# Three of four accumulation banks stream their moving columns in another order

## The chip, the cores and the metric

The kernel runs on one core of one Trainium2 chip. The core has TensorE (PE, which multiplies a weight tile that it loads against moving columns that it streams), VectorE (DVE), ScalarE (ACT), GpSimd (POOL) and SyncE (SP); here the last two mostly issue transfers. SBUF is the working memory of 128 partitions, PSUM holds eight banks of 512 f32 per partition, into which TensorE sums.

The metric is the device time of one execution in microseconds (us). The kernel before takes 709.25 us, the median of three runs (709.15 to 709.4).

## The reference

The reference mixes two branches of a layer on the same input x, of 2048 rows by 512:

```python
a = einsum("bsd,ed->bse", x, dft_hid_re); b = einsum("bsd,ed->bse", x, dft_hid_im)
A = einsum("ts,bse->bte", dft_seq_re, a) - einsum("ts,bse->bte", dft_seq_im, b)
gate = x @ w1; up = x @ w3                  # (2048 x 512) @ (512 x 1376)
B = (silu(gate) * up) @ w2
g = sigmoid((x * gate_w).sum(-1, keepdims=True))
out = g * A + (1 - g) * B
```

All arrays are f32. What matters for the change is the first product of the second branch, gate and up for the first 128 columns of w1 and w3.

## The kernel before, in words

The kernel works in stages. First comes the gate-and-up stage: for each chunk of 128 columns of w1 and w3 it forms silu(x w1) times x w3, transposed, and stores it in DRAM (`hsp`). Then come the products P with the sequence DFT, with w2 and with the hidden DFT, which fill most of the time. Almost all products use a scheme with seven block products in place of eight, whose operands are sums and differences of blocks (T1 to T4 of x, the forms `wa` and `wb` of the weights). Each f32 operand is split in two parts, a high part in the format fp32r, which ScalarE (or once VectorE) makes by a copy (`high`), and a low part, the rest, which VectorE makes by a subtraction (`low`). A product is then three matmuls: high by high, high by low, low by high (`mm3`, line 119).

The instructions of each engine are issued in the order in which the code is written; the kernel asks for a manual schedule, and engines wait for each other by semaphores. Loads go through SyncE's queue, stores mostly through GpSimd's.

The change lies in the very first chunk of the first stage, which is computed undivided: eight block products, no sums, since its operands are then ready as soon as they are loaded. Its result has four blocks, C00, C01, C10 and C11, each 128x512 in a PSUM bank of its own (`C[i, j]`). The first index tells gate (0) from up (1), the second the block of 512 rows of x. The function `half` issues half of one block's sum: six matmuls of 128x128 weights by 128x512 moving columns (line 432), two row blocks times three combinations of high and low. The moving operand is `xp(r, v)`: 512 neighbouring f32 of `XO[0]` (blocks B11, B21, B22 of x) or of the tile `b12`. Every bank gets `half` twice, first with start, then to add.

The order in the code is: eleven warm-up matmuls on a constant (line 407, tile `wps`), splits of the first operands, C00, C10, C00 again, C10 again, C01, C11, C01 again, C11 again, and then the first products X1, Y1, X2 and so on of the divided chunks (`prod1`, `prod2`, line 119). Between them, ScalarE applies Silu to C00 into the tile `s1` (line 466) and to C01 into `g1` (line 482), and VectorE multiplies `s1` by C10 into the first half of `h0` (line 472) and `g1` by C11 into the second (line 490). GpSimd's queue stores each half of `h0` (`store_h`, line 327). On ScalarE and VectorE these four instructions stand between splits (lines 108 and 111) and sums (line 207) of operands that later products need: behind line 466, the splits of the weights of chunks 1 and 2; behind line 472, the sum T2, the low parts `wa` of chunks 1 and 2, and the low part of T2.

Of the kernel before, what the change touches and what calls it, by code (L numbers as in the profile page):

```python
# [9 lines left out]
AF = mybir.ActivationFunctionType  # L10
ALU = mybir.AluOpType

P = 128
# [19 lines left out]
def fnet_swiglu_gate_kernel(  # L33
# [20 lines left out]
    nc = tc.nc  # L54
# [25 lines left out]
    def bank(k, name):  # L80
        return psum.tile([P, 512], F32, tag=f"ps{k}", name=name)
# [131 lines left out]
    def split_xo(g, k):  # L213
        split(*xo_parts(g, k))
# [62 lines left out]
    def prod1(n):  # L277
        x = bank(n % 4, f"X{n}")
        prod(x, n, 0, 0, True)
        return x  # L280
# [41 lines left out]
    def store_h(n, k, h):  # L322

        c, g = ITEMS[n]
        j = min(c % (NP2 - 1) if c < NC - 1 else NP2 - 1, NP2 - 1)
        b = 2 * (NP2 - 1 <= c < NC - 1)
        nc.gpsimd.dma_start(hsp[g, b + k, j // 2, :, j % 2 * 512 : (j % 2 + 1) * 512], h)  # L327
# [90 lines left out]
    b12, a21 = zt[0].rearrange("p h a n -> p h (a n)"), zt[1][:, :, 0]  # L418
    C = {(i, j): bank((0, 4, 6, 7)[2 * i + j], f"C{i}{j}") for i in range(2) for j in range(2)}

    def half(i, j, w, x, start):

        wp = lambda h, sl: a21[:, h, sl] if w is None else WA[0][:, h, w, sl]
        xp = lambda q, h: b12[:, h, q * 512 : (q + 1) * 512] if x is None else XO[0][:, h, x, q, :]
        hh, lh, hl = (0, 0), (1, 0), (0, 1)
        order = [(r, *p) for r in range(2) for p in ((hh, hl, lh) if w is None else (hh, lh, hl))]
        if w == x == 0:
            order = [(r, *p) for some in ((hh, lh), (hl,)) for r in range(2) for p in some]  # L430
        for n, (r, u, v) in enumerate(order):
            nc.tensor.matmul(C[i, j], wp(u, slice(r * P, (r + 1) * P)), xp(r, v),  # L432
                             start=start and n == 0, stop=not start and n == 5)

    def xo_half(k, q):
# [3 lines left out]
    s1 = s1p.tile([P, 512], F32, tag="s1", name="s1_0")  # L439
    g1 = u4p.tile([P, 512], F32, tag="u4", name="g1_0")  # L440
    h0 = hp.tile([P, 1024], F32, tag="h", name="h0")
# [10 lines left out]
    split_by_both(*xo_half("B11", 0))  # L452
    split(*xo_half("B11", 1))
    half(0, 0, 0, 0, True)
    split(a21[:, 0], a21[:, 1], WS[0][:, 3])
    half(1, 0, None, 0, True)
    high(*wa_parts(0, 1, 3)[::2])
    low(*wa_parts(0, 1, 2))
    split_by_both(*xo_half("B21", 0))
    split(*xo_half("B21", 1))  # L460
    low(*wa_parts(0, 2, 3))
    half(0, 0, 1, 1, False)
    split(b12[:, 0], b12[:, 1], ST[0, "B12"])
    half(1, 0, 2, 1, False)
    split_xo(0, "B22")
    nc.scalar.activation(s1, C[0, 0], AF.Silu)
    half(0, 1, 0, None, True)
    WS.pop(0)
    load_w(4)
    sum_xo(0, "T1", t1)  # L470
    half(1, 1, None, None, True)
    nc.vector.tensor_mul(h0[:, :512], s1, C[1, 0])
    store_h(0, 0, h0[:, :512])
    sum_xo(0, "T2", ST[0, "B11"])
    half(0, 1, 1, 2, False)
# [3 lines left out]
    half(1, 1, 2, 2, False)  # L479
    free(*zt)  # L480
    split_xo(0, "T2")
    nc.scalar.activation(g1, C[0, 1], AF.Silu)
    x1 = prod1(1)
    sums_wb(1)
    high(*xo_parts(0, "T1")[::2])
# [99 lines left out]
    for n in range(NI):  # L585
        if n in W2_AT:
            p = W2_AT.index(n)
# [4 lines left out]
        if n in A1_AT:  # L592
            p = A1_AT.index(n)
# [9 lines left out]
    n = NI - 1 - LOOK  # L603
# [348 lines left out]
    for i, (src, sp, p) in enumerate(late):  # L952
        blk, b = 1 + i // 2, i % 2
        n = (17, 24)[b]
# [84 lines left out]
```

## Time and profile before

| | |
|---|---|
| median of three runs | 709.25 us |
| profiled execution, first to last instruction | 707.2 us |
| TensorE busy | 702.7 us, 99% of the span |
| VectorE busy | 605.3 us, 86% |
| ScalarE busy | 370.1 us, 52% |
| instructions of TensorE | 3089 matmuls and as many weight loads |
| share of line 432 in the chain that ended last | 2% |
| mean granted TensorE clock | 0.999 of full |

The page of the profile prints the span of the profiled execution and no other time of it. The chain that ended last follows the work back from the last instruction to what released it. The duration printed for one matmul runs until its modelled end and overlaps the next one; the distance of two starts tells how long the engine is taken up. "C<-xo,wa" is an instruction that writes tile C and reads `xo` and `wa`; PEld is the weight load, which overlaps the matmul before it.

### The profile page before, as it was taken

What the parts mean: (1) busy time and instruction counts of PE and PEld (TensorE: products, weight loads), DVE (VectorE), ACT (ScalarE), POOL (GpSimd) and SP (SyncE); (2) the same over time, 40 slices, a digit from 0 to 9 for tenths busy, and PEclk for the clock granted to TensorE, in tenths of its full rate; (3) what the DMA queues carried; (4) which work ended last, traced back from release to release, by engine and by line L of the source; (5) the groups of instructions that cost most, each with busy time, mean ns of one, the idle gap of its engine ahead of it and who ended that gap; (6) DMA issues with size and microseconds to landing.
All of it is one profiled execution on the core that took longest, in us unless ns stands there. A gap on an engine that the chain in (4) does not pass through costs nothing.

```text
span 707.2 us, 8607 instructions
## 1 busy us (share of the span) xinstructions
PE 702.7 (99%) x3089; PEld 579.2 (82%) x3089; DVE 605.3 (86%) x737; ACT 370.1 (52%) x480; POOL 64.2 (9%) x118
## 2 busy tenths in 40 slices
PE   9999999999999999999999999999999999999997
PEld 6888888888888888888888888888888888888886
DVE  7989978887679999877999689969997896898985
ACT  6666555655446754454554454544555454455452
POOL 0011111211010000000110001100110000000000
PEclk9999999999999999999999999999999999999999
DMA  7665546589997566712595238914999971873932
GB/s 282 239 261 228 214 181 255 184 320 352 419 410 273 212 208 237 277 60 89 181 388 220 90 131 322 335 59 180 389 418 416 355 272 53 301 286 134 320 120 89
DMA packets 45547, 172.54 MB, mean 244 GB/s; under 512 B 5312, under 2 KB 5696, under 8 KB 41664
## 3 DMA queue, kind: packets, MB, share of 16 engines
q1 hardware_dynamic: 32608, 118.63, 45.7%
q0 software_dynamic: 12608, 52.97, 18.9%
q8 instruction: 24, 0.39, 0.2%
q10 hardware_dynamic: 288, 0.39, 0.2%
q14 instruction: 19, 0.16, 0.1%
HBM read 114.82 MB, written 57.16 MB: 243 GB/s over the span
## 4 chain that ended last, share of the span: by engine, by line
PE 99%; DVE 0%; ACT 0%; issue 0%
PE P L119 69%; PE X L119 16%; PE Z L119 8%; PE Y L119 4%; PE C L432 2%; PE wps L407 1%; DVE zc L829 0%; ACT zc L827 0%
## 5 line engine op out<-in xcount | busy, mean ns | idle before, releaser
L119 PE MATMUL P<-zo,a 128*128 128x512 f32 x1344 | 304.8, 389 | 0.0
L119 PEld LDWEIGHTS P<-zo,a 128*128 128x128 f32 x1344 | 252.3, 188 | 52.4
L108 ACT ACTIVATE zo<-B 128x1024 fp32r<-128x1024 f32 (+1 forms) x182 | 189.6, 1045 | 190.6 <-PE P L119 101.2
L111 DVE TENSOR_TENSOR zo<-B,zo 128x1024 fp32r<-128x1024 f32 (+1 forms) x182 | 218.0, 1204 | 48.7 <-ACT zo L108 48.2
L119 PE MATMUL P<-zo,H 128*128 128x512 f32 x468 | 106.2, 389 | 0.0
L119 PEld LDWEIGHTS P<-zo,H 128*128 128x128 f32 x468 | 87.8, 188 | 18.2
L675 DVE TENSOR_TENSOR B<-B,B 128x1024 f32<-128x1024 f32 (+1 forms) x78 | 92.9, 1191 | 0.1
L119 PE MATMUL X<-xo,wb 128*128 128x512 f32 x378 | 92.7, 389 | 0.0
L119 PEld LDWEIGHTS X<-xo,wb 128*128 128x128 f32 x378 | 70.9, 188 | 14.7
L119 PE MATMUL P<-zo,Y 128*128 128x512 f32 x336 | 76.3, 389 | 0.0
L119 PEld LDWEIGHTS P<-zo,Y 128*128 128x128 f32 x336 | 63.1, 188 | 13.1
L327 POOL DMA_DIRECT2D hsp<-h x42 | 23.1, 550 | 127.3 <-DVE h L381 76.1
L119 PE MATMUL X<-xo,wa 128*128 128x512 f32 x126 | 32.0, 389 | 0.0
L119 PE MATMUL Y<-xo,wa 128*128 128x512 f32 x126 | 32.0, 389 | 0.0
L119 PE MATMUL Z<-xo,wb 128*128 128x512 f32 x126 | 32.0, 389 | 0.0
L119 PE MATMUL Z<-xo,wa 128*128 128x512 f32 x126 | 32.0, 389 | 0.0
L678 DVE TENSOR_TENSOR B<-B,B 128x1024 f32<-128x1024 f32 x26 | 31.7, 1220 | 0.0
L904 ACT ACTIVATE zu<-P 128x512 f32<-128x512 f32 x32 | 19.1, 598 | 20.4 <-PE P L119 20.4
L375 DVE TENSOR_TENSOR u<-u,X 128x512 f32<-128x512 f32 x21 | 14.4, 688 | 16.8 <-PE X L119 16.8
L119 PEld LDWEIGHTS Y<-xo,wa 128*128 128x128 f32 x126 | 23.6, 188 | 4.9
L119 PEld LDWEIGHTS X<-xo,wa 128*128 128x128 f32 x126 | 23.6, 188 | 4.9
L119 PEld LDWEIGHTS Z<-xo,wb 128*128 128x128 f32 x126 | 23.6, 188 | 4.9
(137 smaller groups left out, 552.2 us busy)
## 6 DMA issues: line engine op xcount, KB each, us to landing
B<-cc SPq DMA_DIRECT2D x64, 512.0 KB, 6.3
hsp<-h POOLq DMA_DIRECT2D x42, 256.0 KB, 3.6
B<-hsp SPq DMA_DIRECT2D x20, 512.0 KB, 10.5
wbsp<-wb POOLq DMA_DIRECT2D x8, 1024.0 KB, 4.2
wb<-wbsp SPq DMA_DIRECT2D x8, 1024.0 KB, 7.5
B<-zsp SPq DMA_DIRECT2D x16, 512.0 KB, 8.4
H<-w2sp SPq DMA_DIRECT2D x6, 1024.0 KB, 9.2
ws<-w SPq DMA_DIRECT2D x11, 512.0 KB, 5.2
```

What stands on the lines that cost most here:

```text
L108: nc.scalar.activation(hi, src, AF.Copy)
L111: nc.vector.tensor_sub(lo, src, hi.bitcast(F32))
L119: nc.tensor.matmul(ps, u, v, start=first and n == 0, stop=last and n == 2, skip_group_check=chain)
L327: nc.gpsimd.dma_start(hsp[g, b + k, j // 2, :, j % 2 * 512 : (j % 2 + 1) * 512], h)
L375: nc.vector.tensor_add(u4, u4, x)
L407: nc.tensor.matmul(wps, warm[:, :P], warm, start=True, stop=True)
L432: nc.tensor.matmul(C[i, j], wp(u, slice(r * P, (r + 1) * P)), xp(r, v), start=start and n == 0, stop=not start and n == 5)
L675: nc.vector.tensor_add(t, t, RAW[blk, b, q][:, :n])
L678: nc.vector.tensor_sub(t, RAW[blk, "B12", q], t)
L904: nc.scalar.activation(U[name][:, r], ps[r], AF.Copy)
```

## The change

A bank no longer holds its 512 columns in their natural order. For three of the four banks, the matmul streams the moving columns in another order (`ordered`), and writes them into the bank one after another as they come. The view of the bank (`held`) is only a matching shape, and its addresses still run from front to back.

- C00: halves by turns. Columns 0, 256, 1, 257, and so on: each step is 256 elements (1024 bytes) forwards or 255 back.
- C10: even, then odd. Columns 0, 2, 4, ..., 510, then 1, 3, 5, ..., 511: a step of 8 bytes.
- C01: runs of 16 columns, that is 64 bytes, by turns from the first and the second half: 0 to 15, 256 to 271, 16 to 31, and so on.
- C11: as before.

The instructions that read these banks put the columns back: the Silu of C00 and the Silu of C01 write `s1` and `g1` in the order of the bank, so that these tiles are natural again, and the multiply with C10 reads `s1` and writes `h0` in the order even, then odd. The weights, the number of matmuls and their sequence stay.

```diff
+    ORDERS = {(0, 0): ("p (a n) -> p n a", "p (n a) -> p n a", {"a": 2}),
+              (1, 0): ("p (n a) -> p a n", "p (a n) -> p a n", {"a": 2}),
+              (0, 1): ("p (a b n) -> p b a n", "p (b a n) -> p b a n", {"a": 2, "n": 16})}
+
+    def ordered(i, j, v):
+
+        f = ORDERS.get((i, j))
+        return v.rearrange(f[0], **f[2]) if f else v
+
+    def held(i, j):
+        f = ORDERS.get((i, j))
+        return C[i, j].rearrange(f[1], **f[2]) if f else C[i, j]
+
...
-            nc.tensor.matmul(C[i, j], wp(u, slice(r * P, (r + 1) * P)), xp(r, v),
+            nc.tensor.matmul(held(i, j), wp(u, slice(r * P, (r + 1) * P)), ordered(i, j, xp(r, v)),
                              start=start and n == 0, stop=not start and n == 5)
...
-    nc.scalar.activation(s1, C[0, 0], AF.Silu)
+    nc.scalar.activation(ordered(0, 0, s1), held(0, 0), AF.Silu)
...
-    nc.vector.tensor_mul(h0[:, :512], s1, C[1, 0])
+    nc.vector.tensor_mul(ordered(1, 0, h0[:, :512]), ordered(1, 0, s1), held(1, 0))
...
-    nc.scalar.activation(g1, C[0, 1], AF.Silu)
+    nc.scalar.activation(ordered(0, 1, g1), held(0, 1), AF.Silu)
```

## The prediction

> **What bounds the kernel now.** I read the page first for the busy shares and the chain, then the waits of the TensorE side, then the chain in order of time over the first 30 us, then the instructions of the first undivided chunk one by one.
>
> ```profile
> span 707.2 us, 8607 instructions
> ...
> PE 702.7 (99%) x3089; PEld 579.2 (82%) x3089; DVE 605.3 (86%) x737; ACT 370.1 (52%) x480; POOL 64.2 (9%) x118
> ...
> PE 99%; DVE 0%; ACT 0%; issue 0%
> ...
> PEld L407 <- issue: 3.3, 10, 0.7
> PEld C L432 <- ACT xo L108: 0.6, 1, 0.6
> PEld C L432 <- DVE xo L111: 0.2, 1, 0.2
> ```
>
> The chain that ended last is TensorE for 99% of the span. The waits of the weight loads (the last three lines: waiter, releaser, us in total, times, longest) are three in the whole program, all before 7 us: the warm-up, the first matmul of bank C00, and its last. After that no matmul waits for anything. So whatever a matmul of the changed function takes longer goes to the end of the kernel undiminished, and nothing behind it can absorb it.
>
> ```profile
> 0.78 4.85 PE wps L407 x11
> 5.63 11.04 PE C L432 x48
> 16.67 1.36 PE X L119 x6
> ...
> 27.55 2.49 PE X L119 x11
> ```
>
> This is the chain in order of time (start, us, what; the last line is cut by its window). Six matmuls of 128x512 f32 take 1.36 us, so one follows another at 227 ns, here as everywhere. The 48 of line 432 take 11.04 us, 230 ns each. The duration of 389 ns that the groups print for one is its latency, and overlaps its neighbours; the spacing is the price.
>
> **The span against the time.** The sum is made against the profiled span of 707.2 us; the page prints no other time for that execution. The median of the three runs, 709.25, lies 2.05 us above it, and I keep those 2.05 us as they are: the change touches neither the launch nor the end.
>
> **The change part by part.** No instruction, wait, DMA or queue entry is added, removed or moved. Three things change: the addresses from which 36 matmuls stream their moving columns (12 for each of C00, C10, C01; C11 keeps its order), the addresses to which two Silu activations write, and all SBUF addresses of one multiply. The matmuls go on writing their PSUM bank front to back, since only the meaning of the columns changes, and the two activations and the multiply go on reading the bank front to back.
>
> *The matmuls.* Their places in time (start, us, engine, line, operation, out<-in, shapes, count), taken from narrow and wide windows of the timeline:
>
> ```profile
> 5.30 0.66 PE L432 MATMUL C<-xo,wa 128*128 128x512 f32 x1
> ...
> 5.80 0.62 PE L432 MATMUL C<-xo,wa 128*128 128x512 f32 x2
> ...
> 6.71 0.42 PE L432 MATMUL C<-xo,wa 128*128 128x512 f32 x1
> ...
> 6.96 0.62 PE L432 MATMUL C<-xo,a 128*128 128x512 f32 x2
> ...
> 8.34 2.88 PE L432 MATMUL C<-xo,wa 128*128 128x512 f32 x12
> 11.06 1.52 PE L432 MATMUL C<-b,wa 128*128 128x512 f32 x6
> 12.42 1.52 PE L432 MATMUL C<-b,a 128*128 128x512 f32 x6
> 13.78 2.88 PE L432 MATMUL C<-xo,wa 128*128 128x512 f32 x12
> ```
>
> In the order of the code these are: C00 (5.30 to 6.71), C10 (6.96), C00 and C10 again (8.34), C01 (11.06), C11 (12.42), C01 and C11 again (13.78). What a matmul costs when its moving columns are not neighbours no row of this trace shows: every moving operand of the kernel is read in runs of 512 neighbours. So I bound it.
>
> Lower bound. The warm-up matmuls show the array at half its later pace:
>
> ```profile
> 1.16 0.15 PEld L407 LDWEIGHTS <-const-bfloat16-1.0 128*128 128x128 bf16 x1 [0.28 <-issue]
> ...
> 4.57 0.15 PEld L407 LDWEIGHTS <-const-bfloat16-1.0 128*128 128x128 bf16 x1 [0.28 <-issue]
> ```
>
> Eight steps in 3.41 us are 426 ns each; half of that, 213 ns, is the least I can take from rows for 512 columns. Against 227 ns, 14 ns for each of 36 matmuls could be had at most if the spacing held some reading stall that another order avoids: -0.5 us. I see no reason for such a stall, and take no gain.
>
> Upper bound. If a fetch always brings four neighbouring columns and the contiguous stream of 227 ns is already limited by fetches, evens and odds would use half of each fetch (454 ns) and halves by turns a quarter (908 ns), while 64-byte runs (16 columns) would use all. That is +681 ns for a C00 matmul and +227 ns for a C10 one.
>
> What I take for each order, by the row it is nearest to:
> - C00, halves by turns: each column lies 1024 bytes from the one before it, nothing fetched beside a column is wanted next. This is as far from the contiguous rows as an order can be, so the half-paced row is nearer: 426 to 454 ns (the warm-up step, and twice 227), taken as 440, +213 ns each.
> - C10, evens and then odds: a steady walk in one direction with a step of 8 bytes. I take the contiguous row, 227 ns, +0; the upper value is +227 ns.
> - C01, runs of 16 columns by turns: 31 jumps in 512 columns. The contiguous row again, +0; the upper value, should each such pattern halve the pace, is +213 ns.
>
> How many of the 12 count: the first C00 matmul starts at 5.30 and the second at 5.80, so the first already has 500 ns, more than 440, and its extra is covered. Eleven remain: five in the first round and six in the second. Of the wait on VectorE before the sixth (0.2 us on the weight load) only 25 ns reach the matmuls: 6.71 to 6.96 is 250 ns against 227. The sum for C00 is 11 x 213 - 25 = 2.3 us (11 x 199 - 25 = 2.2 at 426 ns; 12 x 227 = 2.7 with all twelve at twice 227).
>
> [...]
>
> *The two activations and the multiply.* Rows of the timeline by engine, with the stretches around them (in brackets the engine's idle time before, and what ended it):
>
> ```profile
> 9.85 1.06 ACT L108 ACTIVATE xo<-xs_B 128x1024 fp32r<-128x1024 f32 x1 [0.21 <-DMA xs_B<-xt]
> 10.82 0.58 ACT L466 ACTIVATE s<-C 128x512 f32<-128x512 f32 x1
> ...
> 12.43 0.85 ACT L108 ACTIVATE wa<-ws 128x768 fp32r<-128x768 f32 x1 [0.29 <-DMA ws<-w]
> 15.08 1.06 ACT L108 ACTIVATE xo<-xs_B 128x1024 fp32r<-128x1024 f32 x1 [1.80 <-DVE xs_B L207]
> 16.05 0.58 ACT L482 ACTIVATE g<-C 128x512 f32<-128x512 f32 x1
> ...
> 13.23 0.68 DVE L472 TENSOR_TENSOR h<-s,C 128x512 f32<-128x512 f32 x1
> ...
> 14.96 0.95 DVE L111 TENSOR_TENSOR wa<-ws,wa 128x768 fp32r<-128x768 f32 x1
> ...
> 16.73 0.19 PEld L119 LDWEIGHTS X<-xo,wa 128*128 128x128 f32 x1
> ...
> 19.30 0.68 DVE L490 TENSOR_TENSOR h<-g,C 128x512 f32<-128x512 f32 x1
> ```
>
> Bounds for each: its present duration, and twice it, for elements written or read at half the pace. The Silu of C00 (line 466) writes halves by turns: 0.58 to 1.16 us. Behind it stand two splits on ScalarE and then an idle stretch of 1.80 us, which takes the 0.58; the multiply that reads it starts at 13.23 and even 10.82 + 1.16 = 11.98 is before that. The Silu of C01 (line 482) ends at 16.63 or 17.21, its reader on VectorE (line 490) starts at 19.30: covered by 2 us. The multiply of C10 (line 472) is the tightest. VectorE has work back to back there, so +0.68 us shifts the low part of wa1 from 14.96 + 0.95 = 15.91 to 16.6, and its reader, the third weight load of X1, comes at 16.73 with its matmul after it. So even at the upper bound and with TensorE not slowed, some 0.1 us is left; that is the next thing to be late. In my forecast TensorE comes 2.3 us later there, and the multiply itself has to wait for C10, which ends at about 11.06 + 2.3 = 13.4 rather than before 13.23: VectorE shifts by some 0.3 to 0.5 us, TensorE by 2.3, so the cover grows. Similarly the Silu of C00, held until 10.82 only because ScalarE was still on the split that started at 9.85, will wait for its bank (9.70 + 2.3, about 12.2), ScalarE falls back by 1.4 us, less than TensorE does. All three at nothing. DMA issues follow these engines and nothing waits for them at this place.
>
> **Sum.** +2.3 us on the span, to 709.5, and 711.55 us against the median of 709.25 (+0.33%).
>
> **The rivals.**
> - *No order matters* (the other side; the change does nothing to time). The moving port fetches far enough ahead that any order streams at 227 ns. For it: nothing in the trace shows that this stream is near a limit of reading, the spacing of 227 ns is 14 ns over half the warm-up step, that is almost the array's own pace, and in bytes it is 2048 in 227 ns, 9.0 bytes per ns. Against it: no row shows more than that rate, and VectorE and ScalarE show less, so spare width is not shown either. It decides if a C00 matmul stays under 240 ns: +0.0 us, 709.25.
> - *Pairs.* A fetch brings two neighbours, and both halves by turns and evens and odds lose half: 2.3 + 12 x 213 ns = 4.9 us, 714.15. The walk of C10 is regular, which speaks against it; wasted bytes speak for it.
> - *Any pattern halves.* C01 pays too, 2.3 + 24 x 213 = 7.4 us, 716.7. The long runs of C01 speak against.
> - *Four neighbours to a fetch, and the stream already at its limit.* 11 x 681 + 12 x 227 = 10.2 us, 719.45. The 14 ns over half the warm-up step may be the sign of such a limit; nothing else is.
> - *Each newly opened group of four neighbours costs alike.* 512 columns open 128 groups in order, 256 by evens and odds, 512 by turns; at 213 ns for 384 more, 128 more are 71 ns: C10 pays 0.85 us, total 3.2 us, 712.4. [...]
>
> **How the numbers follow.** Only C00 at half pace 0.40 (own range 711.2 to 712.0); no order matters 0.20; pairs 0.15; four to a fetch 0.11; any pattern 0.07; per group 0.05; a gain of up to 0.5 us 0.02. A change under 0.2% (1.4 us) cannot be told from none here. The predicted time is the first case, 711.55. Leaving out the 719.45 and the outer edges, the range runs from 708.9 (the possible gain) to 716.9. All cases but two are slower by more than 0.2%: 0.78, less a little for a C00 price of under 130 ns: 0.77. Within: 0.21, since even the full gain of 0.5 us is within it. Faster: 0.02.
>
> **What would show it.** The spacing of the line 432 matmuls in each of the eight rounds. I expect C10's first round to start at 7.9 rather than 6.96, C00's second at 9.3, C10's second at 11.9, C01 at 13.3, X1 at 18.8 rather than 16.50, and every round of C10, C01 and C11 to keep 1.36 us. The three waits of the weight loads should be joined by none. If line 466 prints about 1.1 us, its writes pay, hidden. The prediction is wrong if C00's second round takes 1.36 us, if C10's takes 2.6, or if X1 waits for VectorE.

## The result, and the profile after

The changed kernel takes 712.21 us, the median of three runs (712.17 to 712.28), against 709.25 us: 1.004 times the time of before, with an interval of 1.0026 to 1.0053. That is 2.96 us slower; 711.55 was forecast. The time and its direction came as forecast, but not from where the forecast put it.

The page of the changed kernel, and its chain in order of time (start, us, what; line 445 is what line 432 was):

```profile
span 710.4 us, 8607 instructions
...
PE 705.9 (99%) x3089; PEld 579.7 (82%) x3089; DVE 605.3 (85%) x737; ACT 370.9 (52%) x480; POOL 64.2 (9%) x118
```

```profile
0.78 4.85 PE wps L407 x11
5.63 14.24 PE C L445 x48
19.87 1.37 PE X L119 x6
```

The span grew by 3.2 us, and the 48 matmuls of the first chunk by 3.20 us, from 11.04 to 14.24. Nothing behind them gave any of it back: X1 follows 3.2 us later than before, and the spacing behind it is 1.36 us for six matmuls again. Which bank it was, the table of windows shows, one window to a round of six matmuls (start and end, length, then busy time of each engine, granted clock, DMA share, GB/s):

```profile
5.42:7.32 1.90, 1.90 (x8) 1.61 (x7) 1.90 (x5) 1.52 (x4) 0.00 (x0) 1.00 1.03 420
7.32:10.01 2.69, 2.69 (x7) 1.23 (x6) 2.31 (x6) 2.13 (x4) 0.00 (x0) 1.00 1.02 414
10.01:11.33 1.32, 1.32 (x8) 1.15 (x6) 1.28 (x2) 0.81 (x1) 0.00 (x0) 1.00 1.06 434
11.33:14.02 2.69, 2.69 (x7) 1.23 (x6) 1.88 (x2) 2.49 (x3) 0.00 (x0) 1.00 0.97 388
14.02:15.48 1.46, 1.46 (x8) 1.16 (x6) 1.17 (x2) 0.00 (x1) 0.16 (x1) 1.00 0.05 20
15.48:16.87 1.39, 1.39 (x7) 1.13 (x6) 1.39 (x2) 0.70 (x1) 0.53 (x1) 1.00 0.22 85
16.87:18.31 1.44, 1.44 (x7) 1.14 (x6) 1.44 (x3) 0.36 (x1) 0.00 (x0) 1.00 0.26 100
18.31:19.71 1.40, 1.40 (x8) 1.13 (x7) 1.37 (x3) 1.20 (x2) 0.00 (x0) 1.00 0.00 0
```

The order is C00, C10, C00, C10, C01, C11, C01, C11. The same view of the first four rounds before:

```profile
5.30:6.96 1.66, 1.66 (x7) 1.32 (x7) 1.61 (x3) 1.40 (x3) 0.00 (x0) 1.00 1.03 410
6.96:8.34 1.38, 1.38 (x7) 1.12 (x6) 1.19 (x3) 0.94 (x3) 0.00 (x0) 1.00 1.00 407
8.34:9.70 1.36, 1.36 (x7) 1.13 (x6) 1.09 (x4) 1.06 (x1) 0.00 (x0) 1.00 1.04 422
9.70:11.06 1.36, 1.36 (x7) 1.13 (x6) 1.31 (x2) 1.21 (x2) 0.00 (x0) 1.00 1.03 410
```

Before, the rounds took 1.66, 1.38 and then six times 1.36 us. Both rounds of C10 (evens and then odds) now take 2.69 us, about 450 ns a matmul where it was 227 to 230: +1.31 and +1.33. The second round of C00 (halves by turns) takes 1.32 us, less than before. C01 (runs of 16) takes 0.10 and 0.08 more, and the unchanged C11 0.03 and 0.04 more. The rest, 0.24 in the first round of C00 and a start 0.12 us later, lies in the start-up: the first three starts of C00 are 0.59 and 0.43 us apart, where they were 0.50 and 0.23 before. The 0.43 us is still the step of the warm-up matmuls (426 ns), and from the fourth matmul on this round runs at 216 ns. The sum is 3.2 us, of which C10 has 2.6.

The instructions that put the columns back, in the timeline of ScalarE and VectorE:

```profile
11.53 1.13 ACT L479 ACTIVATE s<-C 128x512 f32<-128x512 f32 x1 [0.71 <-PE C L445]
...
18.51 0.60 ACT L495 ACTIVATE g<-C 128x512 f32<-128x512 f32 x1 [1.28 <-PE C L445]
...
14.31 0.69 DVE L485 TENSOR_TENSOR h<-s,C 128x512 f32<-128x512 f32 x1 [1.10 <-PE C L445]
```

Writing halves by turns took ScalarE 1.13 us for 0.58, hidden as worked out; runs of 16 cost it nothing to speak of (0.60 for 0.58); a step of 8 bytes cost VectorE nothing (0.69 for 0.68). All three now wait for TensorE.

### The profile page after: what moved, and what is told of

Same layout as the page of the kernel before. It is cut to its first block, busy times and chain, and to the rows that moved or that the text cites. A ratio compares the mean times of both kernels' runs of the same rounds, so it can differ in the third digit from the quotient of the medians.

```text
span 710.4 us, 8607 instructions
## 1 busy us (share of the span) xinstructions
PE 705.9 (99%) x3089; PEld 579.7 (82%) x3089; DVE 605.3 (85%) x737; ACT 370.9 (52%) x480; POOL 64.2 (9%) x118
## 4 chain that ended last, share of the span: by engine, by line
PE 99%; DVE 0%; ACT 0%; issue 0%
PE P L119 69%; PE X L119 16%; PE Z L119 8%; PE Y L119 4%; PE C L445 2%; PE wps L407 1%; DVE zc L842 0%; ACT zc L840 0%
## 5 line engine op out<-in xcount | busy, mean ns | idle before, releaser
L119 PE MATMUL P<-zo,a 128*128 128x512 f32 x1344 | 304.8, 389 | 0.0
```

The costliest lines, as they stand in the source:

```text
L119: nc.tensor.matmul(ps, u, v, start=first and n == 0, stop=last and n == 2, skip_group_check=chain)
```

## The experiments

### One bank at a time

Each of three kernels keeps one entry of the table of orders. This one is for C10; the others have `(0, 0)` and `(0, 1)` in its place.

```diff
+    ORDERS = {k: v for k, v in ORDERS.items() if k == (1, 0)}
```

> Only C00 keeps its order, halves by turns; C10 and C01 are as before. Theory of the prediction (halves by turns stream at half pace): +2.2 to +2.7 us, C00's rounds 2.6 us. New theory, from the trace of the changed kernel (a step of 8 bytes is what halves the pace; turns are free, 1.32 us a round): within 0.3 us of before, C00's second round 1.31 to 1.33 us against 1.36, line of the Silu of C00 still 1.13 us and hidden.

> Only C10 keeps its order, evens and then odds. Theory of the prediction: +0.0. New theory: 12 matmuls at 450 ns against 227, +2.7 us, nearly all of the 2.96 us of the whole change.

> Only C01 keeps its order, runs of 16 columns by turns. Theory of the prediction: +0.0. New theory: 12 matmuls at 240 ns against 227, +0.16 us; if C11 behind it is slowed too, as in the trace of the changed kernel (1.40 against 1.36 a round), +0.24 us.

| | median us (before beside it 709.29) | ratio | interval |
|---|---|---|---|
| C00 alone, halves by turns | 709.22 | 0.9999 | 0.9990 to 1.0008 |
| C10 alone, evens and odds | 711.81 | 1.0037 | 1.0025 to 1.0050 |
| C01 alone, runs of 16 | 709.61 | 1.0003 | 0.9994 to 1.0013 |

The chains of the three, in the same order, print for the first chunk:

```profile
5.75 11.32 PE C L446 x48
```

```profile
5.41 14.13 PE C L446 x48
```

```profile
5.69 11.63 PE C L446 x48
```

These three lengths cannot be set beside the 11.04 us of before, because here the chain comes to the first matmul from ScalarE's split and there from the warm-up. From the start of the first C00 matmul to that of X1 it was 11.20 us before (5.30 to 16.50); it is 11.16, 13.96 and 11.47 in the three. The window of C00's second round, alone:

```profile
8.79:10.08 1.29, 1.29 (x7) 1.14 (x6) 1.07 (x3) 1.07 (x2) 0.00 (x0) 1.00 1.04 419
```

C10 alone has 2.52 of the 2.96 us. C00 alone costs nothing, and its second round takes 1.29 us, where it was 1.36. C01 alone has rounds of 1.44 us, as in the changed kernel; its 0.32 us in the time is within the interval of no change. The idea that halves by turns cost 2.3 us has fallen.

### The price of an order by itself

Two kernels got series of matmuls between the second round of C11 and X1, and the next one a third set. In each series twelve matmuls with one weight tile stream 512 columns of x (or of its bits read as bf16) in one order into a bank that none of C00 to C11 uses.

```diff
+    for name, v in SERIES:
+        t = bank(5, name)
...
+        for n in range(12):
+            nc.tensor.matmul(o, WA[0][:, 0, 0, :P], v, start=True, stop=True)
```

> The kernel before with series of 12 extra matmuls between the second round of C11 and X1, all with one weight tile, that stream 512 columns of x in one order each; the time of the whole is of no interest. In order 227 ns each. Three theories of what a read brings. (1) An aligned pair of columns, with a few pairs held: evens and odds 450, steps of two, three and four 450 each, turns of two 220, swap (0, 2, 1, 3) 227, turns of 4 and 8 free until the held pairs run out, then 450; runs of two 227. (2) Four neighbours, with a few such groups held, and a stream that is at its limit in order: step of two 450, step of three 680, step of four 900, swap 227, turns free until the held groups run out, then up to 900. (3) Two banks by the parity of the column: step of two and four 450, step of three 227, swap 227, turns of 16 and 32 growing to 450. The prediction's own theory (what counts is whether the next column is near): turns 440, runs of 16 and steps of two 227.

> Series of 12 extra matmuls as in the run called series, with other orders, then four copies on ScalarE and four additions on VectorE that read one PSUM bank; the time of the whole is of no interest. If a read brings an aligned pair and two distant pairs are held: turns of two columns stream at 216 ns at every distance, the distance of 257 columns and the near ones (4 to 128 columns) included, and in order stays at 227 to 230. If instead the gain of 11 ns comes from the two walks lying far apart, the near ones show from which distance on: 230 at the small ones. bf16 columns: in order 216; if a read brings 8 bytes, a step of two (4 bytes) is free, steps of three and of four (8 bytes) cost 427 or more; if it brings a pair of columns whatever their size, the step of two costs 427 already. ScalarE: writing turns doubles the copy, as in the changed kernel (1.13 against 0.58 us); reading a bank by evens and odds is open: if PSUM reads are as free as VectorE's strided SBUF reads, 0.59. VectorE: 0.68 to 0.69 for a step of 8 bytes, as in the changed kernel.

The chain of the first kernel shows a series to a line; there is a restart of some 0.3 us in each but the first, since a series starts only when the one before it has ended:

```profile
16.84 2.73 PE one L506 x12
...
19.61 2.87 PE turn_two L506 x12
...
22.53 3.03 PE refa L506 x12
...
25.60 5.73 PE evens_odds L506 x12
...
46.51 5.70 PE step_three L506 x12
...
52.25 5.78 PE step_four L506 x12
...
61.15 3.03 PE swap L506 x12
```

To leave the restart out, the table gives the distance from the start of the second matmul to the start of the last, divided by the ten steps between. For the two series that matter most the rows of the timeline are these (the first row of each series holds two matmuls, and the second of them starts 0.32 or 0.33 us after the first, at 19.93 and 22.86; the last row of `refa` holds two as well, and the later one starts at 25.16):

```profile
19.61 0.70 PE L506 MATMUL turn_two<-xo,wa 128*128 128x512 f32 x2
...
22.09 0.38 PE L506 MATMUL turn_two<-xo,wa 128*128 128x512 f32 x1
...
22.53 0.73 PE L506 MATMUL refa<-xo,wa 128*128 128x512 f32 x2
...
24.93 0.61 PE L506 MATMUL refa<-xo,wa 128*128 128x512 f32 x2
```

So (22.09 - 19.93) / 10 = 216 ns by turns, and (25.16 - 22.86) / 10 = 230 ns in order.

| order of 512 f32 columns | ns a matmul |
|---|---|
| in order, seamless behind the kernel's own matmuls | 227 |
| in order, after a restart | 228 to 233 |
| halves by turns: 0, 256, 1, 257 | 216 |
| turns of two columns 4, 8, 16, 32, 64, 128, 257 or 1024 apart | 215 to 216 |
| swap: 0, 2, 1, 3 | 229 |
| evens and then odds, step of two | 454, 455 |
| step of three, step of four | 453, 460 |
| by turns from 4, 8, 16, 32 places | 283, 489, 434, 433 |
| runs of 2, 4, 8, 16, 64 by turns from two halves | 333, 250, 243, 240, 229 |

A step costs the same whether it is 8, 12 or 16 bytes. That rules out four neighbours to a read with a limit on reads (which wants 680 and 900 for steps of three and four) and two banks by parity (which wants 227 for three). Aligned pairs, a few of them held, come nearest, but they want 227 for the runs of two, where the run shows 333, and nothing above 450, where turns from eight places take 489. And they have no reason for the 11 ns that turns gain, at as little as 4 columns apart but not at 2.

### Every second column

A reading came from the table: what counts is not the step to the next column, but the step from each column of the stream to the next but one. By turns that is one column (4 bytes), and a matmul takes 216 ns; in order it is two (8 bytes), 227 to 233; evens and then odds make it four (16 bytes), 454 and 455; steps of three and four make it six and eight, 453 and 460. This is read off the rows in which that step stays the same, and was then put to orders not yet tried. The sharpest one is 0, 256, 2, 258 (`evens_turned`; `wide_evens_turned` goes 0, 512, 2, 514): no two neighbouring columns follow each other, but every second column of the stream still steps by 8 bytes. `fours_turned` goes 0, 256, 4, 260, and `near_evens` 0, 2, 4, 6, 1, 3, 5, 7.

```diff
+    def evens_turned(v, s):
+        return v.rearrange("p (a n s) -> p s n a", a=2, s=s)
```

> Series as before; the time of the whole is of no interest. [...] Theory B (one reader, aligned pairs of 8 bytes, a few held): evens_turned, wide_evens_turned and fours_turned all 454, near_evens 227 if four pairs are held, else 454. [...]

The chain of this kernel:

```profile
25.60 3.07 PE evens_turned L521 x12
28.72 5.68 PE fours_turned L521 x12
34.44 3.03 PE refa L521 x12
37.51 4.27 PE runs_two L521 x12
41.83 4.35 PE near_evens L521 x12
46.22 3.03 PE wide_evens_turned L521 x12
...
52.40 2.76 PE bf_one L521 x12
55.21 5.99 PE bf_turn_two L521 x12
```

Without the restart, evens_turned takes 233 ns, wide_evens_turned 229, fours_turned 451. The reading wants the pace in order, 227 to 233, for the first two and about 454 for the third; aligned pairs wanted 454 for the first two as well. So theory B has fallen. The reading by every second column is not the whole either: where its step changes within the stream, it gives no price. In near_evens every second column goes to and fro by three or four columns, and a matmul takes 340 ns, close to the runs of two (334), where it goes to and fro by about 256. Turns from four places take 283 ns, where it also goes to and fro by about 256, and runs of 4, 8 and 16 take 250, 243 and 240, where it steps by two, as in order, but for the jump from run to run.

For bf16 the picture is another one. In order 216 ns, a step of two (4 bytes) 226, of three (6 bytes) 340, of four (8 bytes) 452. (One of the twelve matmuls with a step of three is missing from the trace; the 340 counts its place.) Every second column then steps by 4, 8, 12 and 16 bytes, and at 4, 8 and 16 bytes f32 took nearly the same: 216, 227 to 233, and 451 to 455. But by turns 484, far or near, against 216 for the swap and 271 and 227 for runs of two and four, and evens_turned takes 540. So by turns, what gains 11 ns with f32 more than doubles the time with bf16. No reading put forward here explains all of these; for bf16 it stays open.

### The same test inside the kernel

Only C10 has another order here, and it is the one that tells the step to the next column from the step of every second column.

```diff
+    ORDERS = {(1, 0): ("p (a n s) -> p s n a", "p (s n a) -> p s n a", {"a": 2, "s": 2})}
```

> Only C10 has another order: 0, 256, 2, 258 and so on, then the odd columns in the same way. Every column is still 1024 bytes from the one before, and no two neighbouring columns come near each other, but every second column of the stream steps by 8 bytes, as in order. [...] One reader with aligned pairs, or a price on steps that are not to the next column: 12 matmuls at 450 ns, 2.5 to 2.7 us slower, as with evens and odds alone. [...]

709.47 us against 709.30, a ratio of 1.0000 (0.9991 to 1.0009). The windows of C10's first round, of C00's second and of C10's second:

```profile
7.55:8.92 1.37, 1.37 (x7) 1.13 (x6) 1.26 (x4) 0.94 (x2) 0.00 (x0) 1.00 1.01 413
8.92:10.28 1.36, 1.36 (x7) 1.13 (x6) 1.11 (x3) 1.14 (x2) 0.00 (x0) 1.00 1.04 425
10.28:11.64 1.36, 1.36 (x7) 1.13 (x6) 1.31 (x2) 1.36 (x2) 0.00 (x0) 1.00 1.03 416
```

C10 streams at its old pace although nearly every column lies about 1 KB from the last. So the 2.5 us of evens and odds do not come from the step to the next column; what every second column does accounts for both results (steps of 8 bytes, 1.37 and 1.36 us a round; of 16 bytes, 2.69). The multiply that puts the columns back took 1.10 us for 0.68, hidden.

### All matmuls by turns

If turns of two stream at 216 ns, the whole kernel can have them, provided that the banks can be read back for nothing. The run called orders had looked at that too: ScalarE copies a bank read by evens and odds in 597 ns, as in order, and VectorE adds one in 687 ns against 686 (shortest, median and longest of four):

```profile
L528 ACT ACTIVATE s<-read_plain x4: 597/597/597, 77.7 to 79.6; 128x512 f32<-128x512 f32 x4
L528 ACT ACTIVATE s<-read_evens x4: 597/597/597, 84.1 to 85.9; 128x512 f32<-128x512 f32 x4
...
L530 DVE TENSOR_TENSOR s<-s,read_plain x4: 686/686/689, 80.3 to 82.4; 128x512 f32<-128x512 f32 x4
L530 DVE TENSOR_TENSOR s<-s,read_evens x4: 687/687/689, 86.6 to 88.7; 128x512 f32<-128x512 f32 x4
```

Writing turns to SBUF cost ScalarE 1.05 us in that run, and writing and reading them there cost VectorE 1.06. So here every matmul streams halves by turns, and every reader takes the bank by evens and odds and writes in natural order.

```diff
+    def turned(v):
+        return v.rearrange("p (a n) -> p n a", a=2)
+
+    def held(ps):
+        return ps.rearrange("p (n a) -> p n a", a=2)
+
+    def nat(ps):
+        return ps.rearrange("p (n a) -> p a n", a=2)
+
+    def two(v):
+        return v.rearrange("p (a n) -> p a n", a=2)
...
-            nc.tensor.matmul(ps, u, v, start=first and n == 0, stop=last and n == 2,
+            nc.tensor.matmul(held(ps), u, turned(v), start=first and n == 0, stop=last and n == 2,
...
-        nc.scalar.activation(s1, x, AF.Copy)
+        nc.scalar.activation(two(s1), nat(x), AF.Copy)
```

> All 3078 matmuls of the kernel but the warm-up stream their 512 moving columns as halves by turns, and ScalarE and VectorE read every bank by evens and odds, so that all SBUF tiles stay in natural order. From the series: 216 ns for 227 to a matmul, and reads of a bank by evens and odds at the old price (597 and 687 ns). If that holds beside the kernel's other traffic: 3078 x 11 ns = 33 us less, 676 us, somewhat more if matmuls now wait for VectorE, which is then busy nine tenths of the time. If the gain is one of the series alone (one weight tile, quiet engines): 709.

679.41 us, the median of five (678.9 to 680.12), against 709.34: a ratio of 0.958, 0.9567 to 0.9593. It beats both kernels. From its page, its chain and its waits (waiter, releaser, us in total, times, longest):

```profile
span 677.1 us, 8633 instructions
...
L131 PE MATMUL P<-zo,a 128*128 128x512 f32 x1344 | 290.8, 380 | 1.0 <-DVE zo L111 1.0
...
16.32 1.29 PE X L131 x6
17.61 1.30 PE Y L131 x6
...
PEld P L131 <- DVE zo L111: 2.3, 3, 1.1
PEld C L444 <- ACT xo L108: 1.4, 2, 1.2
```

The largest group before, for comparison:

```profile
L119 PE MATMUL P<-zo,a 128*128 128x512 f32 x1344 | 304.8, 389 | 0.0
```

Six matmuls take 1.295 us, 216 ns each. The largest group went from 304.8 to 290.8 us. Of the 33 us forecast, 30 came in both the span and the time. TensorE now waits in some places where it did not: 2.3 us for VectorE's low parts are the largest, and the waits of the weight loads other than the warm-up add up to 5.7 us against 0.8. Of the 5.7, 1.7 belong to the first chunk's wait for its splits, which is as long in other kernels of this case (1.9 in the last one above). VectorE, busy for 89% of this span, is the likely next bound; no run tests that.

## Why the prediction was right or wrong

**The bound and the pass-through: right.** Everything that the first chunk takes longer arrived at the end: 3.20 us in the chain of its 48 matmuls, 3.2 in the span, 2.96 in the time. The last two differ because the 2.05 us that the sum kept between span and time set the profiled execution beside the median of others. Where both figures of one execution are known, they lie 1.7 to 1.8 us apart in every run, so the profiled execution before was some 0.2 to 0.3 us faster than the median.

**C00 at half pace, +2.3 us: wrong.** The step that failed is the choice for each order by the row to which it is nearest, where distance to the next column was taken for the measure. Halves by turns cost nothing behind the start-up: 1.32 us a round, 1.29 alone, 216 ns in the series against 227. The lower bound, a gain of up to 14 ns, was the end that held, for a reason that I had said I did not see.

**C10 at the contiguous pace, +0: wrong, by the same step.** It took nearly the upper value of +227 ns: most of its matmuls 451 to 453 ns, +2.64 us for the 12. These two errors, 2.3 us too much and 2.6 too little, nearly cancel, and so it was luck that 711.55 came close to 712.21. By its own tests the prediction was wrong twice over: it named a second round of C00 at 1.36 us and a round of C10 at 2.6 as what would refute it, and both came, the first even lower, at 1.32. The third sign, a wait of X1 for VectorE, did not come; but the weight loads of the first chunk did get new waits, 2.6 us in all, which the prediction said they would not. No rival had it either: pairs had C10 right and C00 wrong, and so did four to a fetch. A price for each newly opened group gave 712.4, nearer than the forecast, with both banks wrong. The upper bound and these three rivals assumed a fetch of two or four neighbours; no run shows one, and steps of three and four columns cost 453 and 460 ns.

**C01, +0: nearly right.** Runs of 16 take 240 ns, 13 more, in the series and in the kernel; why is not shown. The 0.2 us are at the edge of what the times can tell.

**The activations and the multiply: right.** The Silu of C00 took 1.13 us, the twice that was its upper bound, and was covered; the other two stayed at their price. VectorE waited for C10 as foreseen, but fell back by 1.1 us (14.31 against 13.23), not 0.3 to 0.5, since it was C10 that came late. For the order with a step of 8 bytes VectorE paid nothing (0.69 us for 0.68), where TensorE took 451 to 453 ns for 227.

**Not explained:** why the time of a matmul goes with the step of every second column; no run shows what lies behind it. Nor is it shown why C11, which was not touched, takes 232 ns behind C01 for 227. It is no special effect of C01: in the kernel with C01 alone, the first round of C10, in order and behind the start-up, takes the same 1.395 us as C11 there, and in order after a restart the series took 228 to 233 ns. It also stays open why the array left the warm-up's pace later in the one profile of the changed kernel, which made C00's first round 1.90 us; alone, it took 1.65.

## What to carry to other kernels

In these runs the pace of a matmul went with the order in which its moving columns are read, and f32 (fp32r) columns in order were not the fastest: by turns from two places, 16 to 4096 bytes apart in the series, they streamed at 215 to 216 ns for 227, and a plain step of 8, 12 or 16 bytes cost twice (453 to 460 ns). Where a kernel is bound by such matmuls, let them stream by turns and let the readers of the bank put the columns back, since reading a bank with a step of two was free on both engines (597 ns for 597, 687 for 686) and writing SBUF by turns was not (1.05 us on ScalarE). Do not carry it to bf16, where turns cost 484 ns for 216; and a forecast that lands near the time has shown nothing of its terms until each is looked up in the trace.

## What the runs showed that was not expected

- A contiguous f32 stream of 512 columns is not the fastest: 227 ns, against 216 by turns and 216 for bf16 in order. Over 3078 matmuls this was worth 30 us of 709.
- The price of a step is flat: 454, 453 and 460 ns for steps of two, three and four columns.
- In f32, the time went with the step of every second column wherever that step stayed the same: 0, 256, 2, 258 streams like 0, 1, 2, 3 (229 to 233 ns), and 0, 256, 4, 260 like a plain step (451).
- Turns of two places are free or better (216 ns, 229 for the swap), from four places 283 ns, from eight 489.
- The same order has opposite effects by type: halves by turns 216 ns in f32 and 484 in bf16.
